# Two-axis window attention: the second pair's x transposed straight from the input, its projections in one pass of 96 rows, and a new order of all work

## The chip, the cores and the metric

One core of one Trainium2 chip. The time is that of the device, in microseconds, median of the runs; a profiled execution of the same program gives the trace. The engines are TensorE (PE in the profile), VectorE (DVE), ScalarE (ACT), GpSimd (POOL) and SyncE (SP), which here only issues DMAs.

## The reference

x is an image of 224 x 224 tokens with 96 channels, bf16. One projection gives q, k and v; the first 48 channels of each attend within horizontal stripes of 8 rows, the last 48 within vertical stripes of 8 columns. There are 28 stripes of either kind, each with 8 x 224 = 1792 tokens.

```python
qkv = jnp.einsum('bhwc,cd->bhwd', x, wqkv)
q, k, v = (qkv[..., :C].copy(), qkv[..., C:2 * C].copy(), qkv[..., 2 * C:].copy())
scale = C2 ** (-0.5)
qh = q[..., :C2].reshape(B * nh, sw * W, C2)
...
ah = _softmax(jnp.einsum('bqc,bkc->bqk', qh, kh) * scale, axis=-1)
oh = jnp.einsum('bqk,bkc->bqc', ah, vh).reshape(B, H, W, C2)
...
av = _softmax(jnp.einsum('bqc,bkc->bqk', qv, kv) * scale, axis=-1)
ov = jnp.einsum('bqk,bkc->bqc', av, vv).reshape(B, nw, H, sw, C2)
...
return jnp.einsum('bhwc,cd->bhwd', o, wo)
```

## The kernel before

**Pairs and units.** The 56 stripes are done as 28 pairs (P = 0 to 27, the first 14 horizontal). Stripe w = 0 of a pair lives on partitions 0 to 63, w = 1 on 64 to 127, so a stripe's 48 channels fill a quarter of TensorE's array, and the two stripes fill a diagonal of it: two quarters that share neither rows nor columns. Scores (K by Q, L778) mostly lie on one diagonal, the products with V (L804) on the other, so that two groups of matmuls can run at a time. The queries of a pair are cut into four chunks (three of 512, one of 256); a chunk against 128 keys is a unit (two key tiles at a time for the chunk of 256): 49 units a pair, 1372 in all.

**Two ways to the exponential.** 984 units go to ScalarE: the scores of a unit lie in two neighbouring PSUM banks and one instruction (L824) takes both, 128 x 1024. The other 388 units, the DVE units, go in twos: VectorE turns scores to 16-bit integers whose bits read as bf16 approximate the exponential (I_sb, L844), POOL makes two shifted copies of them (U_sb and E_sb, L849), and TensorE adds three products with V (I, U and E; the last with the scaled copy Vs_sb, L651). A conversion of POOL can be given to VectorE instead.

**Projections.** w_sb holds the weights on 96 rows, w2_sb the same in pieces of 64 rows. Pair 0 has its two x transposed apart: the first by a DMA transpose straight from x (L366), the second on TensorE from a plain load; its K, Q and V take one matmul of 96 rows for each stripe. All other pairs go another way: two DMAs write both stripes' channels side by side to a scratch tensor in device memory, x_blocks (192 channels a token, `blocks`, L411), and two DMA transposes (`load`, L418) read channels 0 to 127 into xa_sb and 64 to 191 into xb_sb. A stripe's 96 channels then lie partly in each, and each projection is the sum of two passes of 64 rows (L535, L637), on one diagonal. In pair 0 the mean of K is subtracted from KT_sb by VectorE (L564, L569); in the others a row of w2_sb for Q is changed instead, through two small additions on POOL (L573, L574), a tiny matmul (L602) and a write to w2_sb (L606). The projections of pair P + 1 are done while pair P runs.

**The order.** Every instruction belongs to a stream, named by a letter, and each stream has its order from the loops. The string SEQ, over 11,000 letters, says from which stream the next instruction comes; with it every engine's queue is fixed. A and a, c are the exponential, the scores and the V products of ScalarE's units; j, b, d and D those of the DVE units; U is a conversion on POOL and u the same on VectorE; f and h are projections, e their copies out of PSUM, x and X loads. The string BANK gives each new PSUM tile one of the eight banks; an instruction waits for the one that freed the bank before.

Before the attention begins, SP issues in this order: the transpose of L366, four loads of w2_sb (L422), `blocks` of pair 1, eight small loads of wo_sb, `load` of pair 1, `blocks` of pair 2. ScalarE's queue issues the plain load for pair 0 (L365) and then the load of w_sb (L370).

Of the kernel before, what the change touches and what calls it, by code (L numbers as in the profile page):

```python
# [10 lines left out]
ALU = mybir.AluOpType  # L11
# [12 lines left out]
def ndc(P, c):  # L24
# [4 lines left out]
    "HiIxIihIiHiIhiiiihIiHiiihxIiiiIhiIiixhhxhxhxhhihHhxihhHhhhhhexhHhhxefHfxHfeexeaaxefAaxeafxAeaaxcebcAajabVccAja"  # L29
    "accbexdAacjacbdAjbcacajxbUAacacjbAjbcacajbxUAacjacbddAjacxacffAUeacacebeDAcaejacDAeacuacfAaafcecAecaacfoAaaeff"  # L30
    "cAceaadkgdfAkfradrXadbdeAdfaDaDejbcfcAcjaUcaXcbecAfadadjdfdfAaDeaDUbDXDfAjdadacebcAdcXdajadbdcADucacacDjbAUcac"
    "ajcbcAccjcaadobdADaDajbffdfAjdaUbadedfAcjacacfcecAbacUacegjcAbcacardjbdAdardadVddjdADbDaDjaDbcAdUcjacacbcdAcja"
    "cacDbDAoaUdadjgdAadarDdrbdDAcdjabUadcDjcAaaccbcDcjbAacacjUccgcAaoadrdbrDgADadarjdfdUAdarcacfecAgacaecfcdAUraDr"
    "aDDbDeAfcacajdbdAdaedadjdbkdAckadjUadbDcDAXXjacaccbcAjcbaaccUjcccAfadoadffADfaDeadbdUeAdgjdacacbrcAarcacfjcdbA"
    "UceacadfjdfAadbdadjbfAXcacaeDUdDdDAXjdadafDcADceabacDUcjAcbacacjbcAcoaacjbAgadadrjfUdfADfaDraddfedAaceacbfVcAe"
    "cacajcbdAdjbadaUddjbAddacajcdDbADaDjaDcbUcdAjacacbccDAjabaccDjUbdAacadjdbcAjadadcbocdAUDdadjagDdAcrDgracacDrcA"
    "brcUacacjcccAaoaddbDgAajdaUdfdrdArbDacaecfcAcjagacUcreADbDaDarDfcAdajdadfdeAUdDadacedcAdbdadjaDbcAXXjackacUbcc"
    "AjbacaccjcccAaadokdbUDAjbadaddgjdbAafrDjacffAUracacecfbcAcaejcacfcAdaudadffeAXdfadeaddDAXbdafjacdDAdeabaDDDjcb"
    "AaUcajcbccDAjacabcjcccAabUdaodffAdfjadadcfeAgadeaDVbDcAracjaccbrcAfdUadjadbdAdeadajcdcdAcacauDbDdADjbDacaUcjDc"
    "AbcacjacDbdAcajbaddUjAcbdadaocdcAdajdagDdDrDAcraUcagDcbArcarcaccjcccAaadodbUdfAjdadadecbADgaDjacfcUcAragracceD"  # L40
    "bAcacarjDfDADardadbdefAdadaeddcjdAbkdakdajDUbDcAXXjacaccbcAjbcacacjccUcAfaoaddffAadeaddbdgAjDUbDacarcjfcAacaeD"
    "rbDfDAjcUacadebdAadadjfdfdfAXaceUacdbdcAXjcdadafcADDeabacUcDjcAbcacajcbccAjabacoAfUdadajdfdfAadaegdfDrADfrVaca"
    "cebAcacjacbcUAecacjacbcdAajaddbdjbdAUddaaDjdDDbADdjacaccbcAduacaccDjcDAbadaoUddAjdddbacajcdAbDadjabDDcADjUcaca"
    "cbcgAcjacaccrcAgraUdadrobdADraDacfjcAdadaecUgcfAdragraccreAadaddbrdfdAdajcacfDeAbDaDaeDdcjAdbkdakdajDUbDAXXcaj"
    "cacbccAjbcacacjccUcAfaodadbdfAfjadaddfeADbUaDeacjgcfcArcarcacbedAfadUadjdfbdAdfjacacdceAXdbacUajDbdAXdDjabaDjD"
    "DDAbcacUajcfcAcaceabcAcccjabadUodfAdfadjaddfADbaeDagcjUbcAcarcajcfcAdradadbedfAVcacaeccjbAdadajcUdcdDAbDaDjaDb"
    "cAdcjacacdbUDcAajcabDoAdadajdgddUADdrDarcacbcAdajbadcDjcDAUcagacfrcArcacacecAbUodaadjdgbdAadrjadbDDArcaUgajcfc"
    "AcarceacfcAcracacbedfAdadjadddddAeabUaDjbdDdAajabDDDDAXXjcacUacbcAcjbacacccjcAfadaodkfUdfAbdaedadgDjADacacrcrc"
    "bAkaUjaccfccbAedajbacfcAjdabUadedfAXdfadjaDdDdAXDafabDedcdAUcajcacbcDAcjDbacajccbAcaUodadfdAjdadadfefAfgaecacf"
    "DrAVDracacbecfAcadaedUdjAabdadjbddcdAcjaDaDbDdDuAacacjDcUDcAbcacjacbcAdcjacaddocAUbaaDjbgDAdardajcdcdArcdUabad"  # L50
    "cjbAcDcajcacDcAagcUoacrbArdaadjgdbdAdarjDagDArdaUcarcfrcAcacaecbcfcAjDaDaDebDAadadjfddfAdeaUdacdcedAbdadjaDbDc"
    "AXXjackacUbccAjbcacaccjcfAaadodfkDfAUbDaedadgdjAdfacacerbcrAacUacjcbdfdAjadadbdeddAacjbdacDdjAXabUaDDdjDbAXcDj"
    "aDabcjcAfacUaccfcfAaceaccccbAoaadUdfjDAadadedffAadaDfbfUceAcacaecfcAceadajdbdVAdjbaDaDDjbADDacacjUdbddAjacgadc"
    "rcAbrcacacdjcUbAcacjacdbDAoadadjcgAUbadrajddcdADdrabadDjDcADgUacarcbrcAacacjcbccAcjaUadodbADajDadggdArbdradUac"
    "rjbcAdadardfdAcjacacfecUAcacaebfccAjadaddDedDAadafbdeDAXXDDDjackacUbcAcajcacbcccAjcfaadokdfUAdfadaedbdgcAjDaDa"
    "dfrdbArdUadaejdbdfAcjcacacbecAdcacajbdcdAXDjaUbaDdjDbAXDDaDjabccAjcacaUcffAcfcaeacccAcboadaUdfjdAgadaedffAdfra"
    "DraDcfUcAeabacecfcAcaeacjcbcAacVjbDaDDjbAdadadjbdUAadjbdaDdcjdcAbcacjaccdUAdbacajbcDDAaoaddjbDAgUDadardjdcdAcd"
    "radabcDAgjDUcacacrbcrAacacjcccAbodaUadjDgbDAardjadfddAragacUecbcAacrjacfccAracadefdUdAdaeaDDfDADDeabadDjbkAddU"
    "dadjabcdcAXXjacaccbcAajcakcbcccjcAUfadaodffAdadeadfgdAcrbecraDaDjfcAUcadeadbdfAdfjadadbcAcfjcacabecAXdUcaDjabd"
    "DdAXDjbadajDDDAcbUcacjacfcAcaceaccbcAoaUaddfjfAgfadeaddfdAraDraDVcfecAabaceccjbAcaUdajdbdAdajdadbDdADjbDaUDacj"  # L60
    "dcAbcacjacbcdAcjacaUbdcDAjbacacjcDbAdaoaddUdddjAcgcaacrcrdcAdabafcjDADDaecaUcDcbAcagjaccAroadardgUdbAdradjadbD"
    "ArDacajcbgAcUjacaccfrcAradaddfedAdfUaedacdDeAdDabaDdjbdDADakjDaUbccAXXjcacacbcAcjbacackjcccUAfadaodfcfAacaedgd"
    "bdrAdfarDaDecjbAUcacajcbdfdAjdabadeDfADfUaDjabDfAXdjadacdecdcAXfaUaDceDcAbcacjacbcAdcjacacdbcoAUaajbcgAdardjad"
    "fdfAfrDaDaedfUdAcaeaccbcfAcjacacbecAcVjbacaDDjbAdaddajdbUdAjbdaaDdDjdcAcdbacajbdUcADcajcacbcDAjaaddoDAbUDacajc"
# [204 lines left out]
def bass_standalone__window_attn_cswin__vision_kernel(  # L269
# [32 lines left out]
    with es:  # L302
# [203 lines left out]
        def prep(P, startup=False):  # L506
# [7 lines left out]
            def kq(kind, c, part=False):  # L514
# [73 lines left out]
                else:  # L588
                    prevk.append(ops[0])
                    if c == NCH - 1:  # L590
                        k_ready[P] = ops[-1] if startup else ops[0]
                        k_early[P] = ops[2] if startup else ops[0]
                        if not startup:
                            ksum_op[P] = ops[-1]
# [340 lines left out]
```

## Time and profile before

| | |
|---|---|
| median of 3 runs | 947.26 us (946.06 to 947.78) |
| the profiled execution's own time | 947.97 us |
| its span in the trace | 945.8 us |
| exponentials on ScalarE | 984, 1034 ns each |
| integer conversions on VectorE (L844) | 776, 684 ns each |
| U and E conversions on POOL / on VectorE | 333, 1900 ns / 55, about 687 ns |
| granted clock of TensorE | 0.998 of full speed |

A row of a time line has the start in us, the time it spans, the engine, the line, the operation, what it writes and reads, and a count; idle time just before it and what ended that stand in brackets. In a row of groups the busy time (overlaps counted once) and the mean duration follow the count, then the engine's idle time ahead of these instructions. PE is matmuls, PEld loads of weights, and a name with q (SPq) is the issue of a DMA by that engine's queue. The matmul of 512 columns has a modelled end: it stands with 0.38 us, and the next on the same quarter starts before that.

### The profile page before, as it was taken

Reading aid. Unit: us, or ns where it says so; the run is one execution under the profiler, and the core shown is the slowest. Engines: PE = TensorE matmul, PEld = TensorE weight load, DVE = VectorE, ACT = ScalarE, POOL = GpSimd, SP = SyncE. Lnnn points to the kernel's source line nnn. Section 1 sums busy time; section 2 is a strip of 40 time slices with the busy share of each in tenths; the row PEclk is TensorE's granted clock in tenths of the full one; section 3 lists DMA queues with packets and bytes.
Section 4 is the critical chain, followed back from the end, with each engine's and each line's share of the span. In section 5 each row is a group of like instructions: output and inputs, shape, how many; then the busy total and the mean of one; then the engine's idle time right before and its main releaser. Section 6 shows DMA issues by size and latency. Waiting matters only on the chain.

```text
span 945.8 us, 48282 instructions
## 1 busy us (share of the span) xinstructions
PE 935.8 (99%) x21770; PEld 641.5 (68%) x21770; DVE 883.1 (93%) x1755; ACT 926.0 (98%) x993; POOL 768.3 (81%) x511
## 2 busy tenths in 40 slices
PE   9999999999999999999999999999999999999997
PEld 4766767776677777667666766666776676677664
DVE  8999999999999999999999999999999999999994
ACT  7999999999999999999999999999999999999996
POOL 3789787888898887888888988887888787888883
PEclk9999999999999999999999999999999999999999
DMA  8804422440442243054210534545364544451112
GB/s 141 138 5 71 72 45 29 71 64 11 71 71 38 37 71 61 14 71 71 50 25 12 91 59 57 90 78 81 50 90 74 82 65 67 80 83 31 31 21 45
DMA packets 253254, 57.09 MB, mean 60 GB/s; under 512 B 252936, under 2 KB 252936, under 8 KB 253048
## 3 DMA queue, kind: packets, MB, share of 16 engines
q1 hardware_dynamic: 251464, 53.47, 36.0%
q8 instruction: 170, 2.79, 1.2%
q10 hardware_dynamic: 1584, 0.55, 0.3%
q14 instruction: 36, 0.29, 0.1%
HBM read 19.13 MB, written 28.21 MB: 50 GB/s over the span
## 4 chain that ended last, share of the span: by engine, by line
PE 97%; DVE 1%; DMA 1%; ACT 0%; issue 0%; POOL 0%; POOLq 0%; ACTq 0%
PE ps L804 50%; PE ps L778 36%; PE ps L535 5%; PE ps L637 4%; PE ps L691 1%; PE ps L725 1%; DMA w_sb<-in_wqkv_dram 1%; DVE I_sb L844 0%; ACT PT L824 0%; PE ps L602 0%; DVE out_sb L736 0%; PE ps L634 0%; POOL out_sb L733 0%; POOLq L302 0%; PE ps L529 0%
## 5 line engine op out<-in xcount | busy, mean ns | idle before, releaser
L824 ACT ACTIVATE PT<-ps 128x1024 bf16<-128x1024 f32 x984 | 922.0, 1034 | 7.6 <-PE ps L778 3.4
L778 PE MATMUL ps<-QT_sb,KT_sb 49*64 49x512 bf16 (+1 forms) x6272 | 740.2, 354 | 0.3
L844 DVE TENSOR_SCALAR I_sb<-ps 128x512 int16<-128x512 f32 x776 | 511.8, 684 | 21.0 <-PE ps L778 15.2
L804 PE MATMUL ps<-PT,V_sb 64*50 64x512 bf16 (+1 forms) x4496 | 498.3, 350 | 0.3 <-issue 0.3
L778 PEld LDWEIGHTS ps<-QT_sb,KT_sb 49*64 49x64 bf16 x6272 | 285.0, 105 | 144.5 <-ACT PT L824 44.4
L849 POOL TENSOR_SCALAR E_sb<-I_sb 128x2048 int16<-128x2048 int16 x168 | 319.1, 1900 | 51.8 <-PE ps L804 32.0
L849 POOL TENSOR_SCALAR U_sb<-I_sb 128x2048 int16<-128x2048 int16 x165 | 313.5, 1900 | 49.8 <-DVE I_sb L844 28.4
L804 PE MATMUL ps<-U_sb,V_sb 64*50 64x512 bf16 (+1 forms) x1776 | 245.3, 350 | 0.0
L804 PEld LDWEIGHTS ps<-PT,V_sb 64*50 64x50 bf16 x4496 | 217.7, 100 | 33.9 <-issue 1.0
L804 PE MATMUL ps<-I_sb,V_sb 64*50 64x512 bf16 (+1 forms) x1776 | 239.6, 352 | 0.2
L804 PE MATMUL ps<-E_sb,Vs_sb 64*50 64x512 bf16 (+1 forms) x1776 | 230.6, 349 | 0.0
L733 POOL TENSOR_TENSOR out_sb<-tmp,Ph_sb 128x480 bf16<-128x480 f32 (+1 forms) x84 | 85.7, 1030 | 26.2 <-DVE tmp L729 8.7
L804 PEld LDWEIGHTS ps<-I_sb,V_sb 64*50 64x50 bf16 x1776 | 80.8, 100 | 32.5 <-PE ps L804 9.3
L804 PEld LDWEIGHTS ps<-U_sb,V_sb 64*50 64x50 bf16 x1776 | 89.3, 100 | 12.5
L804 PEld LDWEIGHTS ps<-E_sb,Vs_sb 64*50 64x50 bf16 x1776 | 88.4, 100 | 13.6 <-issue 0.4
L535 PE MATMUL ps<-xa_sb,w_sb 64*64 64x512 bf16 (+3 forms) x440 | 79.9, 355 | 0.7 <-DMA w_sb<-in_wqkv_dram 0.7
L870 DVE CAST OT_sb<-ps 128x512 bf16<-128x512 f32 x112 | 69.1, 617 | 8.4 <-PE ps L804 7.9
L535 PE MATMUL ps<-xb_sb,w_sb 64*64 64x512 bf16 (+2 forms) x436 | 76.9, 348 | 0.0
L556 DVE TENSOR_SCALAR_CACHE_REDUCE KT_sb<-ps,bias 128x512 bf16<-128x512 f32 x108 | 71.6, 677 | 1.9 <-PE ps L535 1.5
L549 DVE TENSOR_SCALAR QT_sb<-ps 128x512 bf16<-128x512 f32 (+1 forms) x111 | 67.4, 616 | 3.7 <-PE ps L535 2.2
L637 PEld LDWEIGHTS ps<-w_sb,xa_sb 64*64 64x64 bf16 x1512 | 59.5, 109 | 10.9 <-DVE I_sb L844 4.0
L637 PE MATMUL ps<-w_sb,xa_sb 64*64 64x48 bf16 x1512 | 66.6, 187 | 0.1
(68 smaller groups left out, 610.4 us busy)
## 6 DMA issues: line engine op xcount, KB each, us to landing
x_blocks<-in_x_dram SPq DMA_DIRECT2D x54, 336.0 KB
out_dram<-out_sb SPq DMA_DIRECT2D x104, 42.0 KB
out_dram<-out_sb SPq DMA_DIRECT2D x208, 21.0 KB
out_dram<-out_sb SPq DMA_DIRECT2D x22, 24.0 KB
xa_sb<-x_blocks SPq DMA_TRANSPOSE x27, 5.0
xb_sb<-x_blocks SPq DMA_TRANSPOSE x27, 5.5
Ph_sb<-in_x_dram ACTq DMA_DIRECT2D x1, 336.0 KB, 3.3
out_dram<-out_sb ACTq DMA_DIRECT2D x6, 24.0 KB
```

The source lines that it names most:

```text
L535: ins = e.matmul(out_, lhsT=wt, rhs=rhs, start=i == 0, stop=startup or i == 1)
L549: return e.tensor_scalar(dst, src, QS if startup else A128, None, ALU.mult)
L556: return e.tensor_scalar(dst, src, bias[:, 0:1], None, ALU.add, ALU.add, accum_out=acc)
L637: ins = e.matmul(out_, lhsT=(xa_sb, xb_sb)[i][b][o:o + 64, 0, t0:t0 + 64], rhs=w2_sb[o:o + 64, i, wblk(P, "v"), 0:C2], start=i == 0, stop= ...
L691: ins = e.matmul(bk3[to:to + 64, s, :], lhsT=OT_sb[b][o:o + CA, blk * 64:(blk + 1) * 64], rhs=wo_sb[0][o:o + CA, :], start=True, stop=True)
L733: return e.tensor_tensor(res, tmp[t][:, 0:n, :], ph, ALU.add)
L778: ins = e.matmul(bank(t.k)[to:to + 64, i * qs:(i + 1) * qs], lhsT=KT_sb[b][64 * w:64 * w + CA, 64 * k:64 * k + 64], rhs=QT_sb[b][64 * w:64 ...
L804: ins = e.matmul(bank(k_.slot.k)[to:to + CP, 0:qs], lhsT=V_[o:o + 64, k, :], rhs=rhs()[o:o + 64, h * 512 + i * qs:h * 512 + (i + 1) * qs], ...
L824: a = wk.add("A", Op("act", ACT, lambda e: e.activation(split(PT[i % NPT]), two(ts), ACTF.Exp, scale=LN128), qs_ + pt_free.get(i - NPT, [] ...
L844: ds.append(wk.add("j", Op("dve", 0.6, lambda e, t=t, at=at: e.tensor_scalar(I_sb[y][:, at:at + 512], bank(t.k), one, 0.0, ALU.add, ALU.ma ...
L849: fn = lambda e, dst=dst, c=c: e.tensor_scalar(dst[:, 0:m], I_sb[y][:, 0:m], float(c), 1.0, ALU.add, ALU.mult)
L870: k.evac = wk.add("o", Op("dve", 0.07 + qs / 960, lambda e, k=k, b=P % 2, q0=q0, qs=qs: e.tensor_copy(OT_sb[b][:, q0:q0 + qs], bank(k.slot ...
```

## The change

Pair 1 no longer goes through x_blocks. Its two stripes are transposed from x itself, one into xa_sb[1], one into xb_sb[1], on SP's queue right behind pair 0's transpose and ahead of the loads of w2_sb. Wherever the code asked for the first pair (`startup`), it now asks for the first two (`wide`) where that means one pass of 96 rows, the mean taken from KT_sb, and the matching scale of Q; which engine copies out of PSUM stays as it was. `mean` is left out for pair 1. SEQ and BANK are new throughout: 11,321 letters against 11,330, with 5 conversions more on VectorE (60) and 5 fewer on POOL (328). The numbers of exponentials, scores and V products are unchanged.

```diff
 SEQ = (
-    "HiIxIihIiHiIhiiiihIiHiiihxIiiiIhiIiixhhxhxhxhhihHhxihhHhhhhhexhHhhxefHfxHfeexeaaxefAaxeafxAeaaxcebcAajabVccAja"
...
+    "HiIxIihIiHiIihiiihIiHxiiihIiiiIihIiihxhhhxhxhixhHhxihhHhhxhhhehxHhhxefHfxHfeexeaaxefAxaeafxAeaaxcecbAaeaVccAjb"
...
+        for t, j in ((xa_sb, 2), (xb_sb, 3)):
+            x_op[1] = first("sp", 1.3, lambda e, t=t, j=j: e.dma_start_transpose(t[1][:, 0:1, :], bass.AP(x.tensor, x.offset + j * NTOK * C, [[C, NTOK], [1, 128]])),
+                            lat=5.1, dma=s_x[1])
         for i, r0, r1, c0 in ((0, 0, 64, 0), (0, 96, 128, 0), (1, 0, 32, 64), (1, 64, 128, 32)):
...
-        blocks(1, "x")
...
-        load(1, "x")
         blocks(2, "x")
...
+            wide = P < 2
...
-                    for i in range(1 if startup else 2):
+                    for i in range(1 if wide else 2):
                         for w in range(2):
                             out_ = bk[64 * w:64 * w + 64, 0:qs]
-                            if startup:
+                            if wide:
                                 src, wt = (xa_sb, xb_sb)[w][b][0:C, 0, :], w_sb[0:C, wblk(P, kind), :]
...
-                        return e.tensor_scalar(dst, src, QS if startup else A128, None, ALU.mult)
+                        return e.tensor_scalar(dst, src, QS if wide else A128, None, ALU.mult)
...
-                        if not startup:
+                        if not wide:
                             return e.tensor_scalar(dst, src, bias[:, 0:1], None, ALU.add, ALU.add, accum_out=acc)
...
-                    for k0, k1 in ((0, EARLY), (EARLY, NTOK)) if startup else ():
+                    for k0, k1 in ((0, EARLY), (EARLY, NTOK)) if wide else ():
...
-                        k_ready[P] = ops[-1] if startup else ops[0]
-                        k_early[P] = ops[2] if startup else ops[0]
+                        k_ready[P] = ops[-1] if wide else ops[0]
+                        k_early[P] = ops[2] if wide else ops[0]
...
-                cut = [0, n] if startup else [0, 4, 7, n] if k0 == 0 else [n * i // 3 for i in range(4)]
+                cut = [0, n] if wide else [0, 4, 7, n] if k0 == 0 else [n * i // 3 for i in range(4)]
...
-                work = [(kq, "k", c) for c in range(NCH)] + [(vv, 0), (mean,), (kq, "q", 0), (vv, VS), (kq, "q", 1), (vv, 2 * VS), (kq, "q", 2), (kq, "q", 3)]
+                work = [(kq, "k", c) for c in range(NCH)] + [(vv, 0)] + [(mean,)] * (P > 1) + [(kq, "q", 0), (vv, VS), (kq, "q", 1), (vv, 2 * VS), (kq, "q", 2), (kq, "q", 3)]
```

284 lines of the change are left out of this document (142 added, 142 removed).

## The prediction

> **What bounds the kernel now.** I read the page's shares first, then the chain that ended last, then the costliest groups, then ScalarE's time line at both ends of the span.
>
> ```profile
> span 945.8 us, 48282 instructions
> PE 935.8 (99%) x21770; PEld 641.5 (68%) x21770; DVE 883.1 (93%) x1755; ACT 926.0 (98%) x993; POOL 768.3 (81%) x511
> PE 97%; DVE 1%; DMA 1%; ACT 0%; issue 0%; POOL 0%; POOLq 0%; ACTq 0%
> PE ps L804 50%; PE ps L778 36%; PE ps L535 5%; PE ps L637 4%; PE ps L691 1%; PE ps L725 1%; DMA w_sb<-in_wqkv_dram 1%; DVE I_sb L844 0%; ACT PT L824 0%; PE ps L602 0%; DVE out_sb L736 0%; PE ps L634 0%; POOL out_sb L733 0%; POOLq L302 0%; P
> L824 ACT ACTIVATE PT<-ps 128x1024 bf16<-128x1024 f32 x984 | 922.0, 1034 | 7.6 <-PE ps L778 3.4
> L778 PEld LDWEIGHTS ps<-QT_sb,KT_sb 49*64 49x64 bf16 x6272 | 285.0, 105 | 144.5 <-ACT PT L824 44.4
> ```
>
> The chain names TensorE for 97%, but a modelled 99% busy array doesn't prove a limit. Another reading is sharper: ScalarE does 984 exponentials of 1034 ns, which sum to 1017 us, more than the span; they overlap one another. How closely they can follow is seen where many follow without a gap:
>
> ```profile
> 9.57 25.63 ACT L824 ACTIVATE PT<-ps 128x1024 bf16<-128x1024 f32 x27 [0.89 <-PE ps L778]
> 914.37 23.95 ACT L824 ACTIVATE PT<-ps 128x1024 bf16<-128x1024 f32 x26
> 933.49 4.82 ACT L824 ACTIVATE PT<-ps 128x1024 bf16<-128x1024 f32 x5
> ```
>
> The second row gives (23.95 - 1.034) / 25 = 0.917 us from one start to the next. The first exponential starts at 9.57, the last ends at 933.49 + 4.82 = 938.31. At 0.917 the 984 would take 983 x 0.917 + 1.034 = 902.5 us; they take 928.7. So the span is 9.6 us ahead of them, 902.5 of necessary exponentials, **26.2 us lost between them** and 7.5 behind. Both kernels have 984 exponentials. A new order can win at most the 26.2 us, if it leaves the ends alone.
>
> They are lost at scores that come late: 188 loads of weights for scores waited for an exponential, 44.4 us in total. An exponential's two banks take the scores of the exponential two places later: in the listed order that is so for 938 of the 984. One score pair must fit between, and what delays it delays ScalarE.
>
> **The change, part by part.** First the second pair's load. It loses two copies to x_blocks and the two transposes from there, and gets two transposes straight from x, which pass the w2_sb loads, the wo_sb loads and all else in SP's queue behind the first transpose.
>
> ```profile
> 13.02 1.26 SPq L418 DMA_TRANSPOSE xa_sb<-x_blocks  x1
> 14.32 2.30 SPq L418 DMA_TRANSPOSE xb_sb<-x_blocks  x1
> L535 PE MATMUL ps<-xb_sb,w_sb x16: 267/374/376, 21.9 to 37.9; 64*64 64x512 bf16 x12, 64*64 64x256 bf16 x4
> xb_sb<-x_blocks SPq DMA_TRANSPOSE x27, 5.5
> ```
>
> The old pair landed at about 14.32 + 5.5 = 19.8 us, and the first use of it is at 21.9; nobody waited for it. An earlier landing is worth nothing. SP is freed of some 5 us of issuing early on, and there too nobody waits: value 0.
>
> The new place has a cost. The start hangs on one small load:
>
> ```profile
> 1.37 4.97 DMA w_sb<-in_wqkv_dram
> 6.48 1.13 PE ps L535 x9
> 0.74 1.32 SPq L366 DMA_TRANSPOSE xa_sb<-in_x_dram  x1
> 2.12 3.15 SPq L422 DMA_DIRECT2D w_sb<-in_wqkv_dram  x4
> Ph_sb<-in_x_dram ACTq DMA_DIRECT2D x1, 336.0 KB, 3.3
> w_sb<-in_wqkv_dram SPq DMA_DIRECT2D x2, 36.0 KB, 3.5
> xa_sb<-in_x_dram SPq DMA_TRANSPOSE x1, 5.5
> ```
>
> 54 KB from ScalarE's queue take 4.97 us, while 336 KB of the same queue take 3.3 and 36 KB from SP's 3.5; it lands at 6.34, just after the one transpose (0.74 + 5.5 = 6.24). So it seems held by that transpose. Now two more follow directly, where w2_sb loads stood. Lower bound 0 (it still goes ahead of them), upper bound two transposes: xa lands at about 13.02 + 5.0, xb at 19.8, so about 1.9 each, 3.8 in all. I take 0.4: it was issued before them, and has so far shared its last stretch with the w2_sb loads as well.
>
> **Projections in one pass.** In pair 2 a 512-column chunk of K or Q needed four 64-row matmuls, two after each other on one diagonal of the array, while the other diagonal worked on something else. Now it needs two of 96 rows, side by side, which take both diagonals.
>
> ```profile
> L535 PE MATMUL ps<-xa_sb,w_sb 64*64 64x512 bf16 x324 | 62.6, 381 | 0.0
> L535 PE MATMUL ps<-xa_sb,w_sb 96*64 96x512 bf16 x6 | 1.9, 382 | 0.7 <-DMA w_sb<-in_wqkv_dram 0.7
> 8.91 0.62 PE L778 MATMUL ps<-QT_sb,KT_sb 49*64 49x512 bf16 x4
> 9.46 0.11 PEld L634 LDWEIGHTS ps<-w_sb,xa_sb 96*64 96x64 bf16 x1 [0.41 <-issue]
> 9.70 0.19 PE L634 MATMUL ps<-w_sb,xa_sb 96*64 96x48 bf16 x1
> 9.82 0.71 PE L778 MATMUL ps<-QT_sb,KT_sb 49*64 49x512 bf16 x4
> ```
>
> 381 against 382 ns: a wide matmul is no shorter. Half as many on twice the array is the same area: gain 0. What comes on top is the change between 96-row and 64-row work. The four scores from 8.91 last 0.62; the last pair started at 8.91 + 0.62 - 0.38 = 9.15, which is 0.24 after the first; another 0.24 gives 9.39, and the wide work came at 9.46. The last of it started at 9.70 and the scores at 9.82. About 0.1 us for each change. The old list has 7 places at which the two kinds meet, the new one 17: 10 x 0.1 = **1.0 us**. Bounds 0 (hidden where TensorE waits anyway) and 2.3 (each like the 0.23 that the trace shows as idle before wide work at 10.46):
>
> ```profile
> 10.46 0.11 PEld L535 LDWEIGHTS ps<-xa_sb,w_sb 96*64 96x64 bf16 x1 [0.23 <-issue]
> ```
>
> **VectorE and POOL.** The mean of K is taken from KT_sb itself in this pair, and five conversions move from POOL to VectorE (60 in place of 55 in the list).
>
> ```profile
> L569 DVE TENSOR_SCALAR KT_sb<-KT_sb,negmean 128x1536 bf16<-128x1536 bf16 x1 | 0.6, 620 | 0.0
> L569 DVE TENSOR_SCALAR KT_sb<-KT_sb,negmean 128x256 bf16<-128x256 bf16 x1 | 0.3, 286 | 0.0
> L606 DVE TENSOR_SCALAR w_sb<-ps x27: 127/156/168, 27.2 to 888.5; 128x2 bf16<-128x2 f32 x27
> L849 DVE TENSOR_SCALAR U_sb<-I_sb 128x2048 int16<-128x2048 int16 x29 | 20.0, 688 | 0.1
> L849 POOL TENSOR_SCALAR E_sb<-I_sb 128x2048 int16<-128x2048 int16 x168 | 319.1, 1900 | 51.8 <-PE ps L804 32.0
> ```
>
> VectorE gets 0.62 + 0.29 - 0.16 + 5 x 0.69 = 4.2 us more, POOL 5 x 1.9 = 9.5 less. VectorE is idle for 945.8 - 883.1 = 62.7 us, which hides most of it. If that cover were gone it would cost the 4.2; the scores of the DVE units and the next K and Q stand behind it in VectorE's queue. I take 0.5. POOL is idle for 177 us: no gain.
>
> **The order.** It is new from end to end, so no step of it can be costed singly; I counted in the two lists what the trace gives a price for. The new list has four exponentials whose scores go into banks that the exponential just before them frees (numbers 38, 39, 494 and 504 of 984); the old one has none. There the next exponential can't start until scores are made: from the row at 8.91 to the exponential at 9.57 it takes 0.66, so it starts 0.66 after its forerunner's end instead of 1.034 - 0.917 = 0.12 before it: 0.78 each, 3.1 in all. Bounds 0 (where ScalarE would be late anyway) and 3.1; I take three of four, **2.3**. For the rest, runs of three and more matmul groups on one diagonal are much more frequent (groups beyond the second of a run: 783 against 239). The array doesn't need strict alternation, though:
>
> ```profile
> 270.75 0.38 PE L804 MATMUL ps<-E_sb,Vs_sb 64*50 64x512 bf16 x2
> 270.85 0.38 PE L778 MATMUL ps<-QT_sb,KT_sb 49*64 49x512 bf16 x2
> 270.96 0.38 PE L804 MATMUL ps<-E_sb,Vs_sb 64*50 64x512 bf16 x2
> 271.18 0.38 PE L804 MATMUL ps<-U_sb,V_sb 64*50 64x512 bf16 x2
> ```
>
> The list has both E products ahead of these scores, and the scores, on the other diagonal, start between them. So a run costs little as long as it is short; I put 0 on it, with bounds of -26.2 (all of ScalarE's lost time regained) and +66 (a rival below).
>
> The sum: 0.4 + 1.0 + 0.5 + 2.3 = 4.2 us. The profiled execution took 947.97 with a span of 945.8, 2.2 around it; it would become 950.0 of span and 952.2. The median of the runs is 947.26, 0.7 below the profiled one, so I forecast **951.5**, with 948.5 to 957 as its own range.
>
> **The rivals.** (1) Faster: the new order brings the scores in time more often. For it: 277 of the 983 distances between exponentials (first and last quoted above) are over 0.937, so the loss is many small delays, which an order can mend. In the new list 522 exponentials have both halves of their scores side by side, so that nothing foreign stands between them (106 before). Against it: in the old run the mean loss ahead of an exponential with its halves side by side was 27 ns, and 25 with one group between them: no better. If a third is regained, 26.2 / 3 = 8.7 less the 1.9 of the other terms: 940.5. Chance 0.34.
>
> (2) No change: the four direct waits fall where ScalarE would have been late anyway and VectorE's and the array's extra work is hidden: 947.3. Chance 0.12.
>
> (3) The load of w_sb comes behind both new transposes: everything shifts by 3.8 in place of 0.4, so 954.9; it decides from the moment at which the first projection starts after 7.5 us in place of 6.48. For it: the 4.97 against 3.3. Against: it was issued first. Chance 0.06.
>
> (4) Slower by far: the array takes groups only in listed order, and each one of a run beyond a neighbour pair stands alone. Pairing neighbours of different diagonals in each list leaves 4179 steps before and 4485 after; 306 more at 0.216 (270.96 to 271.18) are 66 us: 1013.
>
> Against it stands the row at 270.85, which started before one listed ahead of it, as 594 groups of some 7200 do. By the Trainium skill, page "TensorE: Matmul & The Clock Gate", section "Part 3: Packing small matmuls — row/col tiling", matmuls start and end strictly in program order, only weight loads are pulled ahead; by that rule this rival would hold. The trace disagrees with it at 270.85. Chance 0.04, for a window that is too short for the new runs.
>
> **How the numbers follow.** The forecast has 0.44, the rivals 0.34, 0.12, 0.06 and 0.04. A change under 0.2% (1.9 us) can't be told from none here. Slower: 0.44 + 0.06 + 0.04 = 0.54; same 0.12; faster 0.34. The range goes down to 935, which leaves out a regain of more than half of the 26.2 (some 0.09), and up to 962, which leaves out rival 4 and an order that loses 10 us more than I count (0.10 together).
>
> **What would show it.** Right: the first projection at 6.5 to 7.3; the exponentials from first start to last end some 931 to 933 us; gaps of about 0.8 at the 38th, 39th, 494th and 504th. Wrong: fewer than 926 us from first to last exponential (rival 1); a first projection after 7.5 (rival 3); TensorE with many idle stretches on one diagonal and ScalarE's idle time in tens of us (rival 4). If no exponential waits at the four places, my price for them is wrong.

## The result, and the profile after

The changed kernel took 950.78 us (949.63 to 953.02), the kernel before 948.03 us in the runs beside it (945.96 to 949.9): a ratio of 1.0033, with a 95% interval of 1.0024 to 1.0043. It is slower, by 2.75 us; forecast were 951.5 us and 4.2 us more. Of all executions below, one (of the second placing of the wide work) took 3325 us and is left out of its ratio.

From the page of the changed kernel, the span, the shares, and the two groups that were shown of before:

```profile
span 948.8 us, 48134 instructions
PE 939.6 (99%) x21694; PEld 652.9 (69%) x21694; DVE 888.2 (94%) x1763; ACT 924.7 (97%) x993; POOL 758.6 (80%) x504
L826 ACT ACTIVATE PT<-ps 128x1024 bf16<-128x1024 f32 x984 | 920.6, 1037 | 10.8 <-PE ps L780 7.3
L780 PEld LDWEIGHTS ps<-QT_sb,KT_sb 49*64 49x64 bf16 x6272 | 282.5, 105 | 139.0 <-ACT PT L826 41.9
```

VectorE has 5.1 us more work than before and POOL 9.7 less; 4.2 and 9.5 were counted. Loads of weights for scores waited less for an exponential in all (41.9 us, 44.4 before), yet ScalarE stood idle 10.8 us ahead of exponentials, 7.6 before. Where, is seen in its time line. Each row is a stretch of exponentials without a gap, so the numbers of the exponentials come from adding the counts (14, then 14 + 24 = 38, counted from 0):

```profile
10.01 13.38 ACT L826 ACTIVATE PT<-ps 128x1024 bf16<-128x1024 f32 x14 [0.89 <-PE ps L780]
24.04 22.15 ACT L826 ACTIVATE PT<-ps 128x1024 bf16<-128x1024 f32 x24 [0.65 <-PE ps L780]
46.78 1.02 ACT L826 ACTIVATE PT<-ps 128x1024 bf16<-128x1024 f32 x1 [0.59 <-PE ps L780]
48.30 12.45 ACT L826 ACTIVATE PT<-ps 128x1024 bf16<-128x1024 f32 x13 [0.50 <-PE ps L780]
...
475.98 9.27 ACT L826 ACTIVATE PT<-ps 128x1024 bf16<-128x1024 f32 x10 [0.50 <-PE ps L780]
485.75 19.64 ACT L826 ACTIVATE PT<-ps 128x1024 bf16<-128x1024 f32 x21 [0.50 <-PE ps L780]
...
926.65 13.86 ACT L826 ACTIVATE PT<-ps 128x1024 bf16<-128x1024 f32 x15 [0.19 <-PE ps L780]
```

The gaps at the 38th, 39th, 494th and 504th are there, 0.50 to 0.59 us of idle time each. Since exponentials overlap by 1.034 - 0.917 = 0.12, a gap costs that much more than its idle time: 0.70, 0.60, 0.61 and 0.66, together 2.57 us. A fifth, at the 14th, was not foreseen (0.79). From the first start to the last end it is 926.65 + 13.86 - 10.01 = 930.5 us, 928.7 before.

In what follows, **loss** is the sum over neighbouring exponentials of the distance of their starts less 0.917 us, worked out from all 984 starts of a trace; the end is the span behind the last exponential:

| profiled run | first projection | loss, 13th to 35th | 35th to 70th | 490th to 560th | all | end |
|---|---|---|---|---|---|---|
| before | 6.48 | 0.5 | 0.6 | 2.1 | 26.2 | 7.5 |
| after | 6.92 | 0.8 | 2.0 | 2.9 | 28.0 | 8.3 |

The 26.2 of before hold a gap of 0.95 us at the 248th exponential (0.84 of it idle time, at 243.68). The same list with other banks, in the run with twenty direct waits below, loses 0.36 there, so most of it is chance; without it the loss is 25.3. So against the traces' 3.0 us (945.8 to 948.8) stand 0.4 at the start, 1.7 between exponentials (2.7 without that gap) and 0.8 at the end.

### The profile page after: what moved, and what is told of

Its sections match the earlier page's. It is cut to its first block, busy times and chain, and to the rows that moved or that the text cites. A ratio compares the mean times of both kernels' runs of the same rounds, so it can differ in the third digit from the quotient of the medians.

```text
span 948.8 us, 48134 instructions
## 1 busy us (share of the span) xinstructions
PE 939.6 (99%) x21694; PEld 652.9 (69%) x21694; DVE 888.2 (94%) x1763; ACT 924.7 (97%) x993; POOL 758.6 (80%) x504
## 4 chain that ended last, share of the span: by engine, by line
PE 97%; DVE 1%; ACT 1%; issue 0%
PE ps L806 49%; PE ps L780 36%; PE ps L537 5%; PE ps L639 4%; PE ps L727 1%; PE ps L693 1%; ACT PT L826 1%; DVE I_sb L846 1%; PE ps L396 0%; PE ps L636 0%; DVE QT_sb L551 0%; PE ps L497 0%; DVE OT_sb L872 0%; DVE KT_sb L558 0%; DVE out_sb L738 0%
## 5 line engine op out<-in xcount | busy, mean ns | idle before, releaser
L826 ACT ACTIVATE PT<-ps 128x1024 bf16<-128x1024 f32 x984 | 920.6, 1037 | 10.8 <-PE ps L780 7.3
L806 PE MATMUL ps<-PT,V_sb 64*50 64x512 bf16 (+1 forms) x4496 | 527.6, 350 | 0.0
L851 POOL TENSOR_SCALAR U_sb<-I_sb 128x2048 int16<-128x2048 int16 x167 | 317.2, 1900 | 82.7 <-DVE I_sb L846 45.5
L780 PEld LDWEIGHTS ps<-QT_sb,KT_sb 49*64 49x64 bf16 x6272 | 282.5, 105 | 139.0 <-ACT PT L826 41.9
L851 POOL TENSOR_SCALAR E_sb<-I_sb 128x2048 int16<-128x2048 int16 x161 | 305.9, 1900 | 49.8 <-PE ps L806 21.0
L806 PE MATMUL ps<-U_sb,V_sb 64*50 64x512 bf16 (+1 forms) x1776 | 257.4, 350 | 0.0
L806 PE MATMUL ps<-E_sb,Vs_sb 64*50 64x512 bf16 (+1 forms) x1776 | 251.6, 350 | 0.0
L806 PE MATMUL ps<-I_sb,V_sb 64*50 64x512 bf16 (+1 forms) x1776 | 247.0, 352 | 0.0
L537 PE MATMUL ps<-xb_sb,w_sb 64*64 64x512 bf16 (+3 forms) x428 | 76.9, 348 | 0.0
L639 PE MATMUL ps<-w_sb,xb_sb 64*64 64x48 bf16 x1456 | 63.9, 186 | 0.0
```

The lines of the kernel that those rows point to most:

```text
L537: ins = e.matmul(out_, lhsT=wt, rhs=rhs, start=i == 0, stop=wide or i == 1)
L639: ins = e.matmul(out_, lhsT=(xa_sb, xb_sb)[i][b][o:o + 64, 0, t0:t0 + 64], rhs=w2_sb[o:o + 64, i, wblk(P, "v"), 0:C2], start=i == 0, stop= ...
L780: ins = e.matmul(bank(t.k)[to:to + 64, i * qs:(i + 1) * qs], lhsT=KT_sb[b][64 * w:64 * w + CA, 64 * k:64 * k + 64], rhs=QT_sb[b][64 * w:64 ...
L806: ins = e.matmul(bank(k_.slot.k)[to:to + CP, 0:qs], lhsT=V_[o:o + 64, k, :], rhs=rhs()[o:o + 64, h * 512 + i * qs:h * 512 + (i + 1) * qs], ...
L826: a = wk.add("A", Op("act", ACT, lambda e: e.activation(split(PT[i % NPT]), two(ts), ACTF.Exp, scale=LN128), qs_ + pt_free.get(i - NPT, [] ...
L851: fn = lambda e, dst=dst, c=c: e.tensor_scalar(dst[:, 0:m], I_sb[y][:, 0:m], float(c), 1.0, ALU.add, ALU.mult)
```

## The experiments

Each time is a median and stands beside runs of the kernel before taken with it: 948.38 us in the first four experiments; 947.79 for the twenty direct waits, the first placing of the wide work and the list of 1027 us; 948.09 for the second placing, the list after that of 1027 us and the longer runs; 947.84 for the exchanges without new runs; 947.52 for the shorter runs.

### The changed code in the order of before

The second pair's load and its 96-row projections are those of the change; the list is that of before, less what this code no longer has, with the work on the mean put right behind the last copy of K.

```diff
-    "accbexdAacjacbdAjbcacajxbUAacacjbAjbcacajxbUAacjacbddAjacxacffAUeacacebeDAcaejacDAeacuacfAaafcecAecaacfoAaaeff"
-    "cAceaadkgdfAkfradrXadbdeAdfaDaDejbcfcAcjaUcaXcbecAfadadjdfdfAaDeaDUbDXDfAjdadacebcAdcXdajadbdcADucacacDjbAUcac"
+    "accbexdAacjacbdAjbcacajxbUAacacjbAjbcacajbUAacjacbddAjacacffAUeacacebeDAcaejacDAeacuacfAaafcecAecaacfoAaaeffcA"
+    "ceeeeaadgdAradrXadbdeAdaDaDjbcfcAcjaUcaXcbecAfadadjddAaDeaDUbDXDfAjdadacebcAdcXdajadbdcADucacacDjbAUcacajcbcAc"
```

> The change's load and one-pass projections in the old order (only pair 1's letters adapted). Theory, terms of the prediction: start 0.4, changes between 96-row and 64-row work 1.0, VectorE 0.5, so 1.9 over before: about 949.9, and no exponential whose scores wait for the one just before it. Rival, the order does it all: 948.0, same as before. Rival, the wide projections do it all: 950.8, same as the change.

It took 950.62, a ratio of 1.0022 (1.0012 to 1.0033), so 1.1 to 3.1 us more: it is not the order alone that makes the change slower, but whether 1.9 us or all of its 2.75 come with the code, this interval doesn't tell. The loss from the 13th to the 35th exponential is 3.7 us where before had 0.5; elsewhere it is as before. This is TensorE's time line there:

```profile
28.46 0.40 PE L806 MATMUL ps<-PT,V_sb 64*50 64x512 bf16 x2
28.79 0.40 PE L537 MATMUL ps<-xa_sb,w_sb 96*64 96x512 bf16 x1
28.79 0.40 PE L537 MATMUL ps<-xb_sb,w_sb 96*64 96x512 bf16 x1
29.13 0.40 PE L806 MATMUL ps<-PT,V_sb 64*50 64x512 bf16 x2
```

Groups of 512 columns follow each other at 0.216 us on a diagonal. Here it is 0.33 up to the wide pair and 0.34 behind it: 0.12 lost at each change between the kinds, close to the 0.1 that was counted. This list has 27 places at which the kinds meet, 20 more than before, all of them in this stretch: 2.4 us of the 3.2. (The list of the change has 17, the 10 more that the prediction counts.) What the rest is, was not isolated (1.1 us of the mean's work stands in VectorE's queue at that place too).

### The new order with the old projections

The code of before, in the list of the changed kernel with the missing letters put in: two more x and k, seven f, the mean's bank.

```diff
-    "eagcAecaraderdbAdadaejdbdDAeaDacUcjbcAacajcbcdAajdaddduAXXaadddcdcdbAacajbcDjADbaajDbDDAcajUcacDcAacacccccAaao"
+    "AaeagcAecaradrkkdbAdadajdbdDAaDacUcjbcAacajcbcdAajdaddduAXXaadddcdcdbAacfajfbcfDjADebaajDbDfDAcajUecacDcAacacc"
```

> The new order with pair 1 as before (x_blocks, two passes of 64 rows, mean by the small matmul), its letters put in where a bank is free. Theory: the four direct waits of 0.6 to 0.8 stay, and the end of the new order, 0.8 longer in the trace, stays: 2.3 to 3.4 over before, 950.3 to 951.4, first exponential at about 9.6. Rival, the wide projections do it all: 948.0.

955.23, a ratio of 1.007 (1.0057 to 1.0082). Neither time that was expected fits. The letters put in cost by themselves (gaps of 1.27 and 0.81 at the 24th and 23rd exponential), so its total isolates nothing. But the gaps at 14, 38, 39, 494 and 504 stand here as well (0.76, 1.30, 0.60, 0.61 and 0.60), though pair 1's projections are in two passes. They belong to the order, not to the one pass.

### The new transposes further back

In the changed kernel, the two transposes issue behind the loads of w2_sb.

```diff
-        for t, j in ((xa_sb, 2), (xb_sb, 3)):
-            x_op[1] = first("sp", 1.3, ...
         for i, r0, r1, c0 in ((0, 0, 64, 0), (0, 96, 128, 0), (1, 0, 32, 64), (1, 64, 128, 32)):
             op_w2 = first("sp", 0.7, ...
+        for t, j in ((xa_sb, 2), (xb_sb, 3)):
+            x_op[1] = first("sp", 1.3, ...
```

> The change with pair 1's two transposes behind the w2_sb loads in SP's queue instead of ahead of them. Theory: the load of w_sb lands up to 0.15 earlier than the 5.1 after its issue, and the rest of the 0.44 by which the first exponential is late comes from the warm-up matmuls, which lasted 4.02 in place of 3.48 and don't depend on this: total 950.4 to 950.8. Rival, the transposes hold up the start: first exponential back at 9.57 and total 950.3.

950.75, a ratio of 1.0025 (1.0016 to 1.0034): no other than the changed kernel, and its first projection came no sooner (7.14 us).

### Other banks at the four places

The changed kernel with 84 digits of BANK changed around the four, so that no exponential gets a bank from its forerunner; at the 38th its scores also stand ahead of two projections.

```diff
-    "16702341067123467023476043256076423576403247603421067234016702341760234670234760432576452307645230467502346750"
+    "16702341067123467023476062345076245376024507625410267214506752140765212671452761432576452307645231467512346751"
```

> The change with other PSUM banks around the four direct waits (exponentials 38, 39, 494, 504) and two score groups moved ahead of two projections at the 38th, so that no exponential's scores wait for the one just before it. Theory: the four gaps (0.70, 0.60, 0.61, 0.66, 2.6 in all) go and the total falls by 2 to 2.6: 948.2 to 948.8. Rival: ScalarE is not the bound there, the time is lost elsewhere, total 950.8.

954.97, a ratio of 1.0065 (1.0053 to 1.0078): slower, and all four gaps grew (1.20 at 38, 0.73 at 39, 0.86 at 494, 1.54 at 504). Both expectations failed. Its time lines of TensorE's weight loads and of ScalarE at the 504th:

```profile
487.80 0.11 PEld L780 LDWEIGHTS ps<-QT_sb,KT_sb 49*64 49x64 bf16 x4 [1.27 <-ACT PT L826]
489.12 6.54 ACT L826 ACTIVATE PT<-ps 128x1024 bf16<-128x1024 f32 x7 [1.38 <-PE ps L780]
```

A score group still waits for an exponential, now for 1.27 us. The likely reading is that banks are short at these places: with other names the late one goes to a group listed further ahead, and what is listed behind that group waits too. No run tests this by itself. So the four gaps were not removed here, and what they cost in the changed kernel is read from its time line alone.

### Twenty direct waits in the kernel before

```diff
-    "53701634576105436703450673045237604572364507632045367245367214536714531673451670345167054316703451067345036704"
+    "53701634576105436703450673045237604572364507632045367245367214536714531673451670345167054314503671067345036704"
```

and the same at nine more places: two neighbouring pairs of banks change places.

> The kernel before with its order untouched; at ten places, far apart, the pairs of banks of two exponentials that follow each other are exchanged, so that twenty exponentials (two at each place: numbers 153 and 155, 234 and 236, 311 and 313 and so on) get both banks of their scores from the exponential just before them. This measures the direct wait by itself. My price, 0.78 us each as the prediction works it out: 20 x 0.78 = 15.6 us, so about 963.5, with twenty gaps of about 0.8 ahead of just these exponentials. The price as the changed kernel's four places showed it, 0.60 to 0.70 each where one bank of the pair is late: 12 to 14 us, 960 to 962. Rival, the wait is hidden where scores are late anyway, or its loss is regained behind it: 948 to 951. The start of this kernel is that of the kernel before: if its first projection comes at 6.7 to 7.0 us instead of 6.48, the start varies by itself and the 0.44 us at the start of the changed kernel isn't due to the change.

963.12, a ratio of 1.0166 (1.0153 to 1.018): 15.3 us more, 0.77 for each of the twenty. ScalarE's time line at the first place (the 152nd and 154th exponential, counted from 0; the expectation counts from 1):

```profile
144.66 8.36 ACT L824 ACTIVATE PT<-ps 128x1024 bf16<-128x1024 f32 x9
153.73 1.94 ACT L824 ACTIVATE PT<-ps 128x1024 bf16<-128x1024 f32 x2 [0.71 <-PE ps L778]
156.38 9.54 ACT L824 ACTIVATE PT<-ps 128x1024 bf16<-128x1024 f32 x10 [0.71 <-PE ps L778]
```

All twenty losses lie between 0.81 and 0.87 us, 16.5 in sum, and little of it is won back: the loss at all other exponentials is 23.7, where the same ones lose 25.1 in before, 24.2 without the chance gap. The price of a direct wait is as argued. These exponentials get both banks from their forerunner; at the changed kernel's four only one of the two banks comes from it, and 0.60 to 0.70 us were lost.

### Wide work placed anew in the old order

The kernel of the first experiment, its list rearranged up to the 44th exponential.

```diff
-    "ceeeeaadgdAradrXadbdeAdaDaDjbcfcAcjaUcaXcbecAfadadjddAaDeaDUbDXDfAjdadacebcAdcXdajadbdcADucacacDjbAUcacajcbcAc"
+    "AdcagefceXddardaedADrAdbaafdAecccebaacjDAUcdbjaeXafdXAadDajDebfadUAaXcbcjedAadacDddAdjDbucacbcaDDcAjaaAjcbcccc"
```

> The 96-row projections in the order of before (as in the earlier run with that order, which lost 3.7 us between the 13th and the 35th exponential where the kernel before lost 0.5), but with the list rearranged up to the 44th exponential, so that wide work stands beside fewer scores and products, and the inserted work on VectorE is spread. Theory, the wide work costs by its place (it loads both diagonals, where the 64-row work loaded one): the loss between the 13th and the 35th falls to 1.5 us or less, and the time to 948 to 949, within 0.1% of before. Rival, it costs by the changes themselves, 0.1 to 0.2 us each, wherever it stands: the loss stays at 2.5 us or more, and the time at 950 to 951.

950.2, a ratio of 1.0036 (1.0021 to 1.005); the loss from the 13th to the 35th was 4.1. The expectation of 948 to 949 failed. This list also had more runs on one diagonal (282 groups beyond the second, where that of the first experiment has 237), so the same was tried again with fewer:

```diff
-    "ceeeeaadgdAradrXadbdeAdaDaDjbcfcAcjaUcaXcbecAfadadjddAaDeaDUbDXDfAjdadacebcAdcXdajadbdcADucacacDjbAUcacajcbcAc"
+    "egerDaAeDafdaAdardAedeecbdacadbAjfcjaaUcXdAbceacjaDUfbdeAdXacdafDbaDaAcdjecjaAadcdDuddUbcaacAAjDbcDacbccacXccc"
```

> The 96-row projections in the order of before, rearranged up to the 44th exponential as in an earlier run (which came to 950.2 and lost 4.1 us between the 13th and the 35th exponential), but without longer runs on one diagonal: 252 groups beyond the second of a run, where the kernel before has 239. Theory, the wide work costs by its place, and the earlier run gave its gain back in runs: the loss between the 13th and 35th falls from 3.7 to 2.5 us or less, 949 to 949.8. Rival, the wide work costs by itself, 0.1 us and more at each change of kind: the loss stays at 3.5 or more and the time at 950.3 to 951.

949.89, a ratio of 1.0024 (1.0015 to 1.0033), with 3.3 us lost there: between the two answers, the time nearer to the theory's, the loss nearer to the rival's. Two ways of placing it did not bring the cost of the wide work down in the old list, while the list of the change has 0.8 in this stretch. But neither list has fewer changes between the kinds: 31 and 29, where the first experiment has 27 and before 7. At 0.12 us each, 2.9 and 2.6 us of the 3.6 and 2.7 that they lose more than before are the changes, so these runs bear out the price of a change and say little on the place.

### The whole list rearranged

First with no regard to runs on one diagonal, on the code of the first experiment:

```diff
-    "accbexdAacjacbdAjbcacajxbUAacacjbAjbcacajbUAacjacbddAjacacffAUeacacebeDAcaejacDAeacuacfAaafcecAecaacfoAaaeffcA"
+    "aabccdacabjdAacjUUacbVAbAjcjaccabjaaAAcbabacxdjcabaAcjdfaAUjaecAfcbceejeaacADDeccaaccfafAaccuecceAaafaoeccfAee"
```

> The kernel of the run before this one, with its whole list rearranged within some 300 letters at a time, and banks chosen anew, so that no exponential but the first few takes its banks from its immediate forerunner and fewer scores come late. Theory, the 26 us lost between the exponentials hang on the order, and a better one exists: first start to last end of the exponentials 922 to 926 us in place of 928.7, 943 to 946 in all, faster than both. Rival, the loss is the array's load, and a gap mended in one place opens in another: 947 us or more.

1027.3, a ratio of 1.0843 (1.0829 to 1.0857), the worst of all, though it has no direct wait. The group of its exponentials shows where the 79 us went:

```profile
L826 ACT ACTIVATE PT<-ps 128x1024 bf16<-128x1024 f32 x984 | 941.3, 1027 | 68.4 <-PE ps L780 38.1
```

ScalarE is idle for 68.4 us ahead of exponentials, at very many places; 38.1 us of it ended with scores. This is the picture of the prediction's last rival: 1365 groups stand beyond the second of a run. But the whole list is another, so the 79 us can't be put to the runs alone. (774 in the next two expectations is the prediction's 783 of the changed kernel, less the runs that end at work on the whole array.) The next list counted them as costly, in the code of before:

```diff
-    "ajcbcAccjcaadobdADaDajbffdfAjdaUbadedfAcjacacfcecAbacUacegjcAbcacardjbdAdardadVddjdADbDaDjaDbcAdUcjacacbcdAcja"
+    "cabjjcccocaAadAdbDDaabAfdfdfjabcajUAedfdcjaaceccfbcaecAacgbcaAcjdrjabrdUdAdadaVjddcdDbDaDAaAUbDdjccaacbcdcjAUc"
```

> The kernel before (its 64-row projections, its loads), with the list of work rearranged from end to end and banks chosen anew, as in the run that came to 1027 us, but with runs of groups on one diagonal of the array counted as costly, since that run had 1365 groups beyond the second of a run, the changed kernel 774 and the kernel before 239; this one has 555, and no exponential but the first few gets its banks from its immediate forerunner. Theory, the order alone can go both ways and the long runs were what made the earlier run slow: 942 to 946 us, faster than both kernels. Rival, runs cost what they cost in that earlier run, (1027 - 948) / (1365 - 239) = 0.07 us for each group beyond the second: 316 more are 22 us, so 970.

959.63, a ratio of 1.0123 (1.011 to 1.0136). Neither number fits; a price of 0.07 us for every group is too high by a factor of two, and my way of arranging the list misses something even so.

### The runs by themselves

In the kernel before, products and scores of VectorE's units change places with neighbours until 626 groups stand beyond the second of a run, 653 letters in all; then the same with 606 letters, but without new runs of three.

```diff
-    "ajcbcAccjcaadobdADaDajbffdfAjdaUbadedfAcjacacfcecAbacUacegjcAbcacardjbdAdardadVddjdADbDaDjaDbcAdUcjacacbcdAcja"
+    "ajcbcAccjcaadobdADaDajbffdfAjdaUbadedfAcjacacfcecAbacUacegjcAbcacardjbdAdardadVddjdAbDDaDjaDbcAdUcjacacbcdAcja"
```

> The kernel before with pairs of neighbouring products and scores of VectorE's units exchanged in TensorE's list, so that groups of one diagonal stand together: groups beyond the second of a run go from 239 to 626, nearly the 774 of the changed kernel. Scores of exponentials, banks and everything else stay. This prices the runs by themselves. The prediction's term for them, 0: 948 to 950, with 1 to 2 for what the exchanges delay. Rival, 0.07 us each as the run of 1027 us suggests: 387 x 0.07 = 27, so 975. Between them, the array looks ahead over a run of three but not of four: there are 97 runs of four and more in place of 46, 51 x 0.216 = 11, so 959.

> The kernel before with 606 letters of products and of scores of VectorE's units exchanged with their neighbours in TensorE's list, in the same way and nearly as many as in the run that lengthened the runs (653 letters, 9.1 us slower), but so that no run of three or more arises: groups beyond the second of a run stay at 239. Theory, it was the long runs that cost the 9.1 us there: 948 to 950 here. Rival, it was the exchanges, which put products and VectorE's scores at other times than the list was made for: 955 or more. Anything between shares the 9.1 us out in proportion.

957.17 (1.01, interval 1.0085 to 1.0115) and 951.06 (1.0033, 1.0021 to 1.0045). The exchanges alone cost 951.06 - 947.84 = 3.2 us, the runs with them 9.1; 653 / 606 x 3.2 = 3.5 of the 9.1 are then the exchanges' and 5.6 the runs', 0.015 us for each of the 387. That shares the exchanges out by their number, which is an assumption. Of the three times expected for the longer runs 959 is nearest, but of its 11 us for runs of four and more only 5.6 are left beside the exchanges. In the profile it is again spread out:

```profile
L824 ACT ACTIVATE PT<-ps 128x1024 bf16<-128x1024 f32 x984 | 927.8, 1033 | 11.4 <-PE ps L778 5.2
```

That is the longer runs' kernel: 11.4 us of idle time ahead of exponentials, 7.6 in before, and the loss is 35.8 against 26.2, so most of it is in distances that are longer by less than the overlap.

Then the opposite, in the changed kernel itself, by exchanges in 572 letters. The expectation speaks of 316 groups; counted in the way that gave the 783, the list that ran has 406:

```diff
-    "ddudAaaffefADaeDadUcAaedabdjbAdadajdbdAacajgbccrAjcbacadrdduADdDjaDaDbdcAcjaaccccbcdAaUacjbccDAajcacDAofffefda"
+    "ddudAaaffefADaeDadUcAaedabdjbAdadajdbdAacajgbccrAjcbacadrdduADdDjaDaDbdcAcjaaccbccdcAaUacjbccDAajcacDAofffefda"
```

> The changed kernel with neighbouring products and scores of VectorE's units exchanged in TensorE's list so that groups of one diagonal stand apart: groups beyond the second of a run go from 783 to 316 (the kernel before has 239). Scores of exponentials, banks and all else stay. The run that lengthened the runs of the kernel before in the same way cost 957.17 - 948.09 = 9.1 us for 387 more, 0.023 us each. Theory A, the runs of the changed kernel cost as much, and its order wins elsewhere what they cost: 467 x 0.023 = 11 us less, about 940, faster than both kernels. Theory B, they cost nothing where they stand in its list, as the prediction has it: 950 to 951. Rival, the exchanges delay products that somebody waits for: over 952.

950.9, a ratio of 1.0039 (1.0026 to 1.0053): what the changed kernel takes. Its loss is 27.8, the four gaps 2.55 in sum. By 0.015 to 0.023 us each the 377 taken out would have brought 6 to 9 us, and the exchanges, at the old list's price, taken back 572 / 606 x 3.2 = 3.0. No gain is seen, so the runs cost less in this list than in the old one. That they cost nothing is not shown, since what exchanges cost in this list was not measured by itself.

## Why the prediction was right

**The direct waits** were the largest term and were right in place and kind: 2.3 counted, 2.57 found at the four, and 0.77 in place of 0.78 for one when measured by itself. The way to the 2.3 was not: three of four at 0.78 were counted, and it is all four at 0.64 in the mean, one bank of two being late. TensorE's and ScalarE's time lines at the 504th show the mechanism: the scores' weights load when the forerunner ends, at 485.25, and the exponential starts half a microsecond later.

```profile
485.30 0.14 PEld L780 LDWEIGHTS ps<-QT_sb,KT_sb 49*64 49x64 bf16 x6 [0.35 <-ACT PT L826]
485.75 1.94 ACT L826 ACTIVATE PT<-ps 128x1024 bf16<-128x1024 f32 x2 [0.50 <-PE ps L780]
```

At the 38th the prediction named only half of the cause. Four wide projections stand in a row there, and its scores couldn't have come before them, whatever their banks:

```profile
45.18 0.40 PE L537 MATMUL ps<-xa_sb,w_sb 96*64 96x512 bf16 x1
45.67 0.38 PE L537 MATMUL ps<-xa_sb,w_sb 96*64 96x512 bf16 x1
45.89 0.27 PE L537 MATMUL ps<-xa_sb,w_sb 96*64 96x256 bf16 x1
46.11 0.30 PE L780 MATMUL ps<-QT_sb,KT_sb 49*64 49x256 bf16 x2
```

In the run with other banks there is no direct wait at the 38th, and a gap of 1.20 us is there all the same; with projections in two passes it is 1.30.

**The projections in one pass and VectorE's work** were counted at 1.0 + 0.5. In the old list they cost 1.1 to 3.1 us, and 0.12 at each change between the kinds, so the price of a change holds there, for twenty of them. In the new list this stretch loses 0.8, nearly all of it ahead of the 14th exponential, where K's projections fill the array before its scores:

```profile
22.61 0.38 PE L537 MATMUL ps<-xa_sb,w_sb 96*64 96x512 bf16 x1 [0.17 <-ACT PT L826]
22.83 0.38 PE L537 MATMUL ps<-xa_sb,w_sb 96*64 96x512 bf16 x1
23.40 0.79 PE L780 MATMUL ps<-QT_sb,KT_sb 49*64 49x512 bf16 x8
24.04 1.02 ACT L826 ACTIVATE PT<-ps 128x1024 bf16<-128x1024 f32 x1 [0.65 <-PE ps L780]
```

With two passes the same list loses 0.76 at the 14th, so this gap is the place in the list and not the one pass. What is left of the term in the new list is near its lower bound, 0. So the price of a change was right, and the term of 1.5 us too large for the list it came with.

**The start** was the step that failed. The trace of after shows the 0.44 us that were forecast as 0.4, but not from the load of w_sb. Here are four starts: the changed kernel, the same loads in the kernel with shorter runs and in the code of the change with the old order, and the loads of before in the kernel with twenty direct waits.

```profile
1.19 4.02 PE L396 MATMUL ps<-warm 128*128 128x512 bf16 x9 [1.19 <-DVE warm L368]
5.01 1.70 PE L497 MATMUL ps<-Ph_sb 112*96 112x112 bf16 x16
6.92 0.40 PE L537 MATMUL ps<-xa_sb,w_sb 96*64 96x512 bf16 x1
```

```profile
1.19 3.58 PE L396 MATMUL ps<-warm 128*128 128x512 bf16 x9 [1.19 <-DVE warm L368]
4.61 0.95 PE L497 MATMUL ps<-Ph_sb 112*96 112x112 bf16 x16
6.51 0.38 PE L537 MATMUL ps<-xa_sb,w_sb 96*64 96x512 bf16 x1 [0.67 <-DMA w_sb<-in_wqkv_dram]
```

```profile
1.37 5.26 DMA w_sb<-in_wqkv_dram
6.76 0.38 PE L537 MATMUL ps<-xa_sb,w_sb 96*64 96x512 bf16 x1 [0.63 <-DMA w_sb<-in_wqkv_dram]
```

```profile
1.19 4.02 PE L396 MATMUL ps<-warm 128*128 128x512 bf16 x9 [1.19 <-DVE warm L368]
5.00 1.52 PE L496 MATMUL ps<-Ph_sb 112*96 112x112 bf16 x16
6.79 0.38 PE L535 MATMUL ps<-xa_sb,w_sb 96*64 96x512 bf16 x1
```

With the new loads the first projection can come at 6.51, and with the old ones at 6.79. In most executions it follows TensorE's own work: nine warm-up matmuls, which take 3.48 to 4.02 us in one execution or another, and sixteen small transposes behind them, which take 0.95 to 1.70. Only in the three runs where these were quickest (before, and the second and third of the starts above) does the load of w_sb end the wait. It lands at 5.9 to 6.4 us in six runs with the old loads and at 6.1 to 6.6 in seven with the new, 0.2 later in the mean, most of which is hidden: the first projection comes at 6.75 and 6.82 in the mean of the same runs, with a spread of 0.5 and 0.7. So the term is nearer to 0.1 than to 0.4, and it fell on the right value by chance. The rival that holds w_sb behind both transposes is out: the load landed at 6.63 at the latest.

**The runs on one diagonal** were put at 0, with 66 us as the far bound. In the changed kernel, taking half of them out won nothing. The reason given, that groups of the free diagonal start ahead of earlier ones, is only half of it: by the exchanges, the same runs cost about 0.015 us apiece in a list not made for them, and the list with the most of them was 79 us slower. The rival of strict order deserved its place, but its 1013 us are out. By the Trainium skill, page "TensorE: Matmul & The Clock Gate", section "Part 3: Packing small matmuls — row/col tiling", matmuls start strictly in program order. The traces disagree: in before 594 of 7202 groups start ahead of one listed earlier (see the last section).

**The end** was not in the sum: 0.8 us. Behind the last exponential SP is still issuing stores of the result, one behind another without a pause: 24 of pair 26, then 22 of pair 27. This is its time line in before and in after:

```profile
912.78 15.55 SPq L760 DMA_DIRECT2D out_dram<-out_sb  x24
928.37 15.67 SPq L749 DMA_DIRECT2D out_dram<-out_sb  x22
```

```profile
915.77 15.54 SPq L762 DMA_DIRECT2D out_dram<-out_sb  x24
931.35 15.67 SPq L751 DMA_DIRECT2D out_dram<-out_sb  x22
```

The 46 issues take 31.3 us in either, and the last one's data is ready more than 2 us before its turn. So the end hangs on when this row begins: 938.31 - 912.78 = 25.53 us ahead of the last exponential's end in before, 940.51 - 915.77 = 24.74 after, a difference of 0.8. It begins as soon as POOL's last addition for pair 26 ends (at 912.75 and 915.74), and the changed list leaves that one later. Kernels with the end of the new list have 8.3 to 9.1 us behind the last exponential (the one of two passes 9.6), those with the old one, or one near it, 7.0 to 8.0.

Of the 3.0 us between the two traces, then, some 2.2 are the four places (2.57 less the 0.33 that before loses there), 0.8 the 14th exponential, 0.8 the end, 0.4 a slow start by chance; less the 0.95 us that one chance gap cost the profiled run of before, and 0.3 that the rest of the list wins. Without the two parts that are chance the traces are 3.5 us apart, the medians 2.75 (2.3 to 4.1), so what lies between is not resolved. The rival that a third of the 26.2 us would be regained is out: 28.0 are lost. So is that of no change. The forecast of 4.2 was 1.5 too high: the changes between the kinds hardly show in the new list, and the start costs next to nothing. That it came this close is in part luck, since the gap at the 14th and the end, 1.6 us that were not in the sum, make up for these.

No kernel here beats the kernel before.

## What to carry to other kernels

A bank that is handed from one exponential straight to the next cost 0.6 to 0.8 us here, nearly a whole cycle of scores, so count the distances between a bank's last reader and its next writer before running a new order. But a late bank isn't renamed away for nothing: in the one try here other waits took its place and grew. Follow the queue that ends last, too: here it was that of the stores, and what starts it lies 25 us ahead of the end. And an order fits the work it was made for: letters moved to make room for other work cost more (3.2 us for 606 neighbours exchanged) than most single operations that one counts.

## What the runs showed of the hardware

Matmul groups on the free diagonal of the array start ahead of groups listed earlier, but by little. In the list of before 594 of 7202 groups start at least 10 ns before one listed ahead of them, in the changed one 1321, in the list of 1027 us 1526 (some 100 more by another way of matching the trace to the list), and never was one found that passed more than three. Behind one group of the other diagonal a group starts 9 to 16 ns after its own diagonal is free, behind two 22 to 69, behind three 74 to 197 (means in before and after, whatever else a group waited for). That may be how runs cost, where somebody waits for just that group; no run isolates it.

Nine equal matmuls at the start take 3.48, 3.58, 3.87 or, in eleven of the fourteen profiled runs, 4.02 us. And seven of these runs have one or two single gaps of 0.9 to 1.5 us where the lists nearest to theirs have none of that size (1.21 at the 600th with the transposes further back, 0 there in after; only the 147th comes twice, in two lists that are the same around it). The four gaps of the changed list come back to within 0.05 us where it is run again with other runs. In the eight single gaps TensorE starts neither a load nor a matmul for 0.95 to 1.45 us. Seven of the eight begin 0.3 to 0.7 us after a transfer of DMA queue q8 has ended, which brings instructions (170 transfers in before, one in some 5.3 us), and the eighth as one ends; most such transfers are followed by no gap. This points at the supply of instructions, but no run tests it.
